# A third two-bank PSUM tile shared by scores and feed-forward units in a block-sparse attention and squared-ReLU kernel

## The chip, the cores and the metric

The kernel runs on one core of a Trainium2 chip. Its time is device microseconds of one execution. The core has a matrix engine (PE), which writes its results to PSUM; a vector engine (DVE) and a scalar engine (ACT), which read PSUM and write SBUF; a general engine (POOL), which works on SBUF; and a sequencer (SP), which issues transfers here. All run in parallel, each takes its own instructions in order, and semaphores order them among each other. PSUM has eight banks of 512 fp32 values per partition.

## The reference

```python
B, H, S, D = q.shape                       # 4, 8, 768, 64; blocks of 32, 24 of them
scores = scale * np.matmul(q, k.transpose(0, 1, 3, 2))
mask = np.abs(blk_i - blk_j) <= 1
mask = mask | (blk_i == 0) | (blk_j == 0) | (blk_i == n_blocks - 1) | (blk_j == n_blocks - 1)
for qb in range(n_blocks):
    for kb in sampled_blocks[qb]:
        mask[qb * block:(qb + 1) * block, kb * block:(kb + 1) * block] = True
scores = np.where(mask, scores, -1000000000.0)
...
x = softmax(scores) @ v                    # softmax written out in the reference
x = x.transpose(0, 2, 1, 3).reshape(B * S, H * D)     # 3072 x 512
h = x @ w_in                               # 512 x 2048
r = np.maximum(h, 0.0)
out = (r * r) @ w_out                      # 2048 x 512, result 3072 x 512
```

## The kernel before

**Attention.** Heads are taken in pairs, so there are 16 units `u` (4 batches of 4 pairs), and keys lie on the partitions. The work is cut into *slots*: a unit, a query tile and a group of key chunks of 128. In batch 0 the first 256 queries are two tiles of 128 with three key chunks per slot (16 slots in all); everywhere else a tile has 256 queries and a slot two key chunks. There are 148 slots. `scores` (L391) fills a slot's two-bank PSUM tile, one bank per head; its matmuls have only 64 rows, one half of the array for each head. In the narrow slots `scores` also adds the mask with a second matmul (L395). `exps` on ACT (L402) takes the tile to SBUF as `pT`; `masks` on DVE (L409) multiplies the 0/1 mask `MK` in; `values` (L431) accumulates `po`, whose 65th column is the softmax's sum; `normalize` (L439, L441) divides; a transpose, on PE in batch 0 and by DMA later, gives `xT`. Queries and keys are cast on DVE, POOL or ACT (L198 to L200) and transposed, on PE for batch 0 (`pt`, L343) and by DMA on SP's queue later (L350). The mask tiles `MK` are made on PE (`pk`, L313) and evacuated by DVE or ACT.

**Feed-forward.** Token tiles of 128, 128, 256 and 256 (batch 0) and of 384 (later) go through `hidden` (L485: `w_in` columns against `xT`, into `ph`), `relu` on ACT or DVE (L492, L494: PSUM to fp32 in SBUF), `square` on POOL or ACT (L503, L501: to bf16) and `output` (L526: into `py`), which ACT or DVE copies out and SP's queue stores. A *unit* of `hidden`, `relu` and `square` is one block of 128 hidden features, or two for the tiles of 128 tokens, so 256 or 384 wide.

**PSUM.** `ps_s` holds two tiles of two banks for scores, `ps_h` two single banks for `ph`, `pk`, `pt` and one in two of the last tile's outputs, `ps_o` one bank for `po`, `ps_y` one for `py`.

**Order.** Nothing runs in the order in which the code states it. Every piece of work is a task (`T_`) with durations per engine, a key, things it waits for, buffers that it takes (`get`) and gives back (`put`). `run_schedule` (L119) plays them on a clock of its own and always issues the task that can start first by that clock, ties by key; keys carry a small pseudo-random part (`TIES`, `SEEDS`). So each engine's order is fixed when the kernel is built, and at run time an engine that waits holds everything behind it. A *visit* is an uninterrupted stretch of score matmuls on PE. `attend` puts two slots in one visit, and in batch 0's narrow tiles one. From batch 1 on a visit isn't planned before a pace (`PACE0`, `PACE`). The weights come in eight pieces over POOL's queue (L365, L368), and two pieces of `w_out` gate batch 1's first loads (`GATES`, L375).

Of the kernel before, what the change touches and what calls it, by code (L numbers as in the profile page):

```python
# [25 lines left out]
def kernel(  # L26
# [27 lines left out]
    TWM = 384  # L54
# [5 lines left out]
    PT_BUFS, R_BUFS, G_BUFS, XT_BUFS = 6, 4, 2 * NF + 2, 3  # L60
# [3 lines left out]
    ps_s = ctx.enter_context(tc.psum_pool(name="ps_s", bufs=2))  # L64
    ps_o = ctx.enter_context(tc.psum_pool(name="ps_o", bufs=1))
    ps_h = ctx.enter_context(tc.psum_pool(name="ps_h", bufs=2))
# [9 lines left out]
    CB, GATES = 0.4, (6, 7)  # L76
    QT0, ADDED, ALONE = [(0, 128), (128, 128), (256, 256), (512, 256)], (0, 128), (0, 128)
# [5 lines left out]
    AHEAD = {"PE": 0.021, "DVE": 0.089, "ACT": 0.144, "POOL": 0.0, "SP": 0.0}  # L83
    LEAD = 9.733
    PACE0, PACE, SINGLE, MASK_AT = 43.352, 1.684, 1, 17.0

    class Buf:
        def __init__(self, pool):
            self.pool, self.holds, self.free = pool, 0, 0.0
# [4 lines left out]
    TIES = 2.757, 2.707  # L94
    SEEDS = (
            997007, 734824, 532673, 925841, 745989, 714641, 109461, 798098, 925326,
            634149, 527289, 224329, 653624, 743444, 608088, 229557, 928387, 381331,
            84432, 104783, 194889, 255966, 621276, 580226, 46894, 921115)
# [6 lines left out]
    class Task:  # L105
        def __init__(self, engs, key, fn, deps=(), get=(), put=(), after=0.0, mode=None, dma=0.0, late=None, bias={}, port=False):
            self.engs = engs if isinstance(engs, dict) else dict([engs])
            self.key, self.fn = key, fn
            self.deps, self.get, self.put = list(deps), list(get), list(put)
            self.after, self.mode, self.dma, self.late, self.bias = after, mode, dma, late, bias  # L110
            self.port = port
            self.end = self.eng = None
            self.order = len(tasks)
            self.key += TIES[0 if key < 300 else 1] * tie(self.order)
            for b in self.put:
                b.holds += 1
            tasks.append(self)

    def run_schedule(free, bufs, dma_free, mode=128):  # L119
        taken = {name: [] for name in bufs}  # L120
        port = {"DVE": (0.0, 0.0), "POOL": (0.0, 0.0)}
# [7 lines left out]

        while waiting or ready:  # L130
            now = [t for t in waiting if all(d.end is not None for d in t.deps)]
# [4 lines left out]
            found, urgent = [], {}  # L136
            for t in ready:
                r0 = t.after
                ok = True
                cnt = {}  # L140
                for b in t.get:
                    held = taken[b.pool]
# [10 lines left out]
                for e, us in t.engs.items():  # L153
                    r = max([r0, free[e]] + [seen(d, e) for d in t.deps])
# [6 lines left out]
                found.append((round(opt[1], 4), t.key, t.order, t, opt))  # L161
                if t.key < 100:
# [3 lines left out]
                       key=lambda c: c[:3], default=None)  # L166
            assert best is not None, "no task can start"
# [19 lines left out]
            for b in t.get:  # L187
                taken[b.pool].append(b)
# [65 lines left out]
    junk = ps_h.tile([P, 512], F32, name="junk", tag="h")  # L254
    for _ in range(N_WARM):
        nc.tensor.matmul(junk[:, 0:256], warm[:, 0:P], warm, start=True, stop=True)
# [45 lines left out]
    def mask_rows(c0, c1, e):  # L302
        mtile["R"] = ps_s.tile([P, 1024], F32, name="pb", tag="ps")[:, 0:c1 - c0]
# [7 lines left out]
    def mask_tile(n, c0, c1, e):  # L311
        pk = ps_h.tile([P, 512], F32, name="pk", tag="h")[:, 0:c1 - c0]
# [26 lines left out]
    def transp(u, w, ns, e):  # L339
        src = cast.pop((u, w, ns.start))  # L340
        pt = ps_h.tile([P, NCH, P], BF, name="pt", tag="h")
# [39 lines left out]
    def scores(slots, add, e):  # L381
        for a in slots:
            u, q0, w, cs = a
            i = u % NPB
            ps = ps_s.tile([P, 2, 512], F32, name="ps", tag="ps")
# [88 lines left out]

    def per_unit(T):
        return 2 if T[2] == P else 1

    def hidden(T, f, half, e):
        b, c0, w = T
        n = per_unit(T)  # L480
        if half == 0:
            htile[T, f] = ps_h.tile([P, TWM], F32, name="ph", tag="h")[:, 0:w * n]
        work_ = [(f + i, i, kc) for i in range(n) for kc in range(KM)]
        for f_, i, kc in work_[half * len(work_) // 2:(half + 1) * len(work_) // 2]:
            nc.tensor.matmul(htile[T, f][:, i * w:(i + 1) * w], w_in_sb[:, kc, f_ * P:(f_ + 1) * P], xT[b][:, kc, c0:c0 + w],  # L485
                             start=(kc == 0), stop=(kc == KM - 1))

    def relu(T, f, e):
        r = work.tile([P, TWM], F32, name="r", tag="r", bufs=R_BUFS)[:, 0:T[2] * per_unit(T)]
        src = htile.pop((T, f))  # L490
        if e == "ACT":
            A.activation(out=r, in_=src, func=AF.Relu)  # L492
        else:
            V.tensor_scalar(out=r, in0=src, scalar1=0.0, scalar2=None, op0=AOP.max)  # L494
        rltile[T, f] = r

    def square(T, f, e):
        g = work.tile([P, TWM], BF, name="g", tag="g", bufs=G_BUFS)[:, 0:T[2] * per_unit(T)]
        r = rltile.pop((T, f))
# [4 lines left out]
        for i in range(per_unit(T)):  # L504
            gtile[T, f + i] = g[:, i * T[2]:(i + 1) * T[2]]
# [12 lines left out]
    def y_pool(T, i):  # L518
        return "h" if T == TILES[-1] and i % 2 else "y"

    def output(T, i, ts, cs, part, e):
        if part == 0:
            pool, tag = (ps_h, "h") if y_pool(T, i) == "h" else (ps_y, "y")
            ytile[T, i] = pool.tile([P, d_model], F32, name="py", tag=tag)[:, 0:cs[1] - cs[0]]
# [14 lines left out]
    def T_(engs, key, f, *args, **kw):  # L539
# [5 lines left out]
              (3, 0, 0): 9.8, (3, 1, 0): 10.9, (1, 2, 0): 11.9, (2, 2, 0): 13.0, (3, 2, 0): 14.0}  # L545
    arrive.update({(u, 0, 2): (15.1, 15.8, 16.4, 17.1)[u] for u in range(HP)})
# [13 lines left out]
    def prepare(u):  # L560
# [17 lines left out]
        else:  # L578
            at = dict(after=arrive[u, 2, 0])
            late_q = first_of_tile[u, 2 * P]  # L580
            for w, ns in [(1, ns) for ns in (KEYS if u == 0 else (ALL,))] + [(0, ns) for ns in QRS]:
# [4 lines left out]
                qc, hb = Buf("qc"), Buf("h")  # L586
# [6 lines left out]
                t = T_(("PE", 0.06 * n), key + 1, transp, u, w, ns, deps=[c], get=[hb], put=[qc], mode=128)  # L593
# [12 lines left out]
    def attend(group, add):  # L606
        s = min(order.index(a) for a in group)
        bufs = {a: Buf("ps") for a in group}
# [3 lines left out]
        sc = T_(("PE", (0.44 if add else 0.22) * area), s, scores, group, add,  # L612
                deps=deps + (mr[:1 + (group[-1][1] + group[-1][2] > QW)] if add else []) + sc_all[-1:], get=[bufs[a] for a in group], mode=64,
                after=PACE0 + PACE * (s - N0) * (1.06 - 0.0006 * (s - N0)) if s >= N0 else 0.0)
        sc_all.append(sc)
        for a in group:
# [5 lines left out]
            ex = T_(("ACT", 0.2 + 0.82 * part), s, exps, a, deps=[sc], get=[pt], put=[bufs[a]])  # L622
# [4 lines left out]
            va = T_(("PE", 0.245 * part), s + 3.009, values, a, deps=[ex] + cv[u] + va_all[-1:] + (kws if po_pool(u, q0) == "y" else []),  # L627
# [23 lines left out]
    for i, (c0, c1) in enumerate(((0, QW), (QW, S))):  # L651
        rb_ = Buf("ps")
        t = T_(("PE", 0.11 + 0.11 * i), 5.0 if i else -90.0, mask_rows, c0, c1, after=9.8 if i else 4.6, get=[rb_], put=[], mode=32)
# [6 lines left out]
    for us in [range(b * HP, (b + 1) * HP) for b in range(B)]:  # L660
# [3 lines left out]
        if us[0] < HP:  # L664
            for c0, c1, at in MASKED:
                for n in range(NCH):
                    mb, w = Buf("h"), (c1 - c0) / 512
                    t = T_(("PE", 0.216 * w), (2 * n + 30 if c0 == 0 else 2 * n + 2), mask_tile, n, c0, c1, get=[mb], mode=128, after=at, deps=mr)
# [3 lines left out]
            while mine:  # L672
                q0 = mine[0][1]
                n = 1 if q0 in ALONE or len(mine) == 1 else 2
                attend(mine[:n], q0 in ADDED)
                mine = mine[n:]
        else:
            for i in range(0, len(mine) - 1, 2):
# [82 lines left out]
```

## Time and profile before

| what | value |
|---|---|
| median of 13 runs (lowest, highest) | 274.0 us (273.22, 276.55) |
| the profiled execution: its own time | 274.45 us |
| its span, first to last instruction | 272.7 us |
| busy: PE, ACT, DVE, POOL | 97%, 76%, 69%, 40% of the span |
| granted PE clock | 1.000 |
| scores to `pT` on ACT (L402), 128x1024 | 132 of 1022 ns |
| mask on DVE (L409) | 132 of 788 ns |
| relu of 384: on ACT (L492), on DVE (L494) | 46 of 497 ns, 50 of 556 ns |
| relu of 256: on ACT, on DVE | 35 of 404 ns, 13 of 420 ns |
| square of 384: on POOL (L503), on ACT (L501) | 62 of 963 ns, 34 of 525 ns |
| square of 256: on POOL, on ACT | 33 of 848 ns, 15 of 430 ns |
| output copy of 512 (L198, L200): on ACT, on DVE | 21 of 589 ns, 2 of 680 ns |

A mean is the length of one instruction from start to reported end. Neighbours on one engine overlap somewhat, so how many fit in a stretch is read from the distance of their starts. The end of a matmul is modelled, so a PE that is busy 97% of the time may still be held up; distances between starts show it.

### The profile page before, as it was taken

What the parts mean: (1) busy time and instruction counts of PE and PEld (TensorE: products, weight loads), DVE (VectorE), ACT (ScalarE), POOL (GpSimd) and SP (SyncE); (2) the same over time, 40 slices, a digit from 0 to 9 for tenths busy, and PEclk for the clock granted to TensorE, in tenths of its full rate; (3) what the DMA queues carried; (4) which work ended last, traced back from release to release, by engine and by line L of the source; (5) the groups of instructions that cost most, each with busy time, mean ns of one, the idle gap of its engine ahead of it and who ended that gap; (6) DMA issues with size and microseconds to landing.
All of it is one profiled execution on the core that took longest, in us unless ns stands there. A gap on an engine that the chain in (4) does not pass through costs nothing.

```text
span 272.7 us, 7435 instructions
## 1 busy us (share of the span) xinstructions
PE 263.6 (97%) x2994; PEld 164.1 (60%) x3032; DVE 189.5 (69%) x380; ACT 207.5 (76%) x321; POOL 110.2 (40%) x138
## 2 busy tenths in 40 slices
PE   8999999999999999999999999999999999999995
PEld 5778766667676555665556555556555555555544
DVE  6698879988786768889667877776666875434400
ACT  3798999999999879999998799889999881010111
POOL 3293453357446126444420270431411414666410
PEclk9999999999999999999999999999999999999999
DMA  6999998999991285399721133255210111111112
GB/s 193 372 225 201 206 279 267 293 295 335 200 231 22 94 140 165 74 258 249 209 58 51 53 76 71 58 108 60 67 52 19 51 20 51 38 40 41 38 71 83
DMA packets 51882, 36.92 MB, mean 135 GB/s; under 512 B 30984, under 2 KB 48904, under 8 KB 51848
## 3 DMA queue, kind: packets, MB, share of 16 engines
q1 hardware_dynamic: 47080, 31.86, 45.2%
q0 software_dynamic: 4224, 4.19, 9.7%
q8 instruction: 23, 0.38, 0.6%
q10 hardware_dynamic: 544, 0.39, 0.5%
q14 instruction: 11, 0.09, 0.1%
HBM read 27.26 MB, written 6.29 MB: 123 GB/s over the span
## 4 chain that ended last, share of the span: by engine, by line
PE 82%; DMA 11%; POOL 2%; ACT 2%; issue 1%; DVE 0%; SPq 0%; ACTq 0%
PE py L526 29%; PE ph L485 29%; PE po L431 12%; PE ps L391 12%; DMA w_out_sb<-in_moe_w_out_dram 6%; DMA vs<-in_v_dram 3%; DMA qs<-in_q_dram 2%; ACT pT L402 1%; POOL w_in_sb L365 1%; POOL w_out_sb L368 1%; ACT ys L198 0%; POOL VT L200 0%; PE pk L313 0%; ACT xT L198 0%; DVE pT L409 0%
## 5 line engine op out<-in xcount | busy, mean ns | idle before, releaser
L402 ACT ACTIVATE pT<-ps 128x1024 bf16<-128x1024 f32 (+1 forms) x148 | 140.2, 1000 | 11.8 <-PE ps L391 7.7
L503 POOL TENSOR_TENSOR g<-r 128x384 bf16<-128x384 f32 (+1 forms) x95 | 87.0, 923 | 121.1 <-DVE r L494 64.3
L409 DVE TENSOR_TENSOR pT<-pT,MK 128x1024 bf16<-128x1024 bf16 x132 | 102.2, 788 | 16.4 <-ACT pT L402 15.9
L485 PE MATMUL ph<-xT,w_in_sb 128*128 128x384 bf16 (+2 forms) x640 | 106.4, 294 | 0.1
L526 PE MATMUL py<-w_out_sb,g 128*128 128x512 bf16 (+1 forms) x362 | 94.2, 370 | 2.6 <-issue 0.5
L485 PEld LDWEIGHTS <-w_in_sb 128*128 128x128 bf16 x640 | 52.0, 97 | 28.7 <-issue 5.0
L431 PEld LDWEIGHTS <-pT 128*128 128x128 bf16 x1152 | 47.3, 98 | 17.3 <-issue 4.1
L494 DVE TENSOR_SCALAR r<-ph 128x384 f32<-128x384 f32 (+1 forms) x63 | 33.1, 528 | 31.4 <-PE ph L485 28.8
L431 PE MATMUL po<-VT,pT 128*128 128x65 bf16 x1152 | 53.7, 193 | 0.5 <-DVE pT L409 0.3
L526 PEld LDWEIGHTS <-g 128*128 128x128 bf16 x400 | 36.2, 98 | 28.6 <-issue 3.1
L391 PE MATMUL ps<-QK 64*128 64x256 bf16 (+1 forms) x624 | 47.6, 265 | 0.6 <-ACT pT L402 0.5
L198 ACT COPY ys<-py 128x512 f32<-128x512 f32 (+1 forms) x23 | 13.1, 570 | 38.0 <-PE py L526 37.8
L391 PEld LDWEIGHTS <-QK 64*128 64x128 bf16 x624 | 25.1, 95 | 23.0 <-issue 19.6
L492 ACT ACTIVATE r<-ph 128x384 f32<-128x384 f32 (+1 forms) x81 | 34.3, 457 | 3.0 <-PE ph L485 2.8
L501 ACT ACTIVATE g<-r 128x384 bf16<-128x384 f32 (+1 forms) x49 | 24.1, 496 | 6.0 <-DVE r L494 4.8
L200 POOL CAST VT<-vs 128x768 bf16<-128x768 f32 x15 | 13.9, 925 | 24.6 <-PE po L431 14.5
L441 DVE TENSOR_TENSOR xq<-po,rs 128x256 bf16<-128x256 f32 (+1 forms) x52 | 21.0, 404 | 1.8
L439 DVE RECIPROCAL rs<-po 128x4 f32<-128x4 f32 (+1 forms) x52 | 9.1, 176 | 13.6 <-PE po L431 13.2
L200 DVE CAST qc<-qs 128x768 bf16<-128x768 f32 (+2 forms) x18 | 11.7, 652 | 0.3 <-DMA qs<-in_q_dram 0.3
L200 DVE CAST qc<-ks 128x768 bf16<-128x768 f32 (+1 forms) x15 | 9.0, 603 | 2.3 <-DMA ks<-in_k_dram 2.2
L395 PE MATMUL ps<-R,oh 64*128 64x128 bf16 x96 | 7.1, 223 | 0.0
L343 PE MATMUL pt<-identb,qc 128*128 128x128 bf16 x48 | 5.3, 234 | 0.7 <-DVE QK L200 0.6
(51 smaller groups left out, 64.0 us busy)
## 6 DMA issues: line engine op xcount, KB each, us to landing
vs<-in_v_dram SPq DMA_DIRECT2D x16, 384.0 KB, 6.7
out_dram<-ys SPq DMA_DIRECT2D x23, 256.0 KB, 2.1
ks<-in_k_dram SPq DMA_DIRECT2D x15, 384.0 KB, 5.1
qs<-in_q_dram SPq DMA_DIRECT2D x12, 384.0 KB, 4.4
w_in_sb<-in_moe_w_in_dram POOLq DMA_DIRECT2D x4, 512.0 KB, 8.8
w_out_sb<-in_moe_w_out_dram POOLq DMA_DIRECT2D x4, 512.0 KB, 16.5
qs<-in_q_dram SPq DMA_DIRECT2D x4, 256.0 KB, 7.3
xT<-xq SPq DMA_TRANSPOSE x36, 2.3
```

What stands on the lines that cost most here:

```text
L200: (V if e == "DVE" else G).tensor_copy(out=out, in_=in_)
L391: nc.tensor.matmul(ps[:, h, j * w:(j + 1) * w], QK[i][hs, 1, ksl], QK[i][hs, 0, qsl], start=j == 0, stop=not add, skip_group_check=True)
L402: A.activation(out=pT[:, :, 0:n], in_=stile.pop(a)[:, :, 0:n], func=AF.Exp, scale=scale)
L409: V.tensor_tensor(out=pT, in0=pT, in1=m[:, None].broadcast_to([P, 2, len(cs), w]), op=AOP.mult)
L431: nc.tensor.matmul(po[:, qc, h, :], pT[:, h, j * w + qc * P:j * w + (qc + 1) * P], VT[i][:, h, n, 0:VW], start=(n == 0 and qc == 0 and h = ...
L441: V.tensor_tensor(out=xq, in0=po[:, :, :, 0:D], in1=rs.broadcast_to([P, n, 2, D]), op=AOP.mult)
L485: nc.tensor.matmul(htile[T, f][:, i * w:(i + 1) * w], w_in_sb[:, kc, f_ * P:(f_ + 1) * P], xT[b][:, kc, c0:c0 + w], start=(kc == 0), stop= ...
L492: A.activation(out=r, in_=src, func=AF.Relu)
L494: V.tensor_scalar(out=r, in0=src, scalar1=0.0, scalar2=None, op0=AOP.max)
L501: A.activation(out=g, in_=r, func=AF.Square)
L503: (G if e == "POOL" else V).tensor_mul(out=g, in0=r, in1=r)
L526: nc.tensor.matmul(ytile[T, i], gtile[T, f][:, ts * P:(ts + 1) * P], w_out_sb[:, f, cs[0]:cs[1]], start=(f == 0), stop=(f == NF - 1))
```

## The change

*PSUM.* `ps_s` and `ps_h` go. There are two tiles X0 and X1 of two banks from the start, and two single banks F0 and F1, which hold the transposes, mask tiles, mask rows and the first two tiles' hidden units in the opening. When no task is left that needs a single bank, F0 and F1 are given up and become a third two-bank tile X2. Scores' slots, hidden units of the other token tiles and every second output of the last tile take any free X tile.

*Units.* A unit is 512 wide in batch 0 (four feature blocks of 128 tokens or two of 256) and 768 later (two of 384), and `relu` takes it in one instruction across two banks. Squares are 512 or, two to a unit, 384 wide. The buffers for squares are still 34, now up to 512 wide instead of 384; the four relu buffers are 768 wide.

*Visits.* `GROUPS` says how many slots a visit has, by batch and query third: (1, 2, 2), (2, 2, 2), (2, 2, 3), (3, 3, 3). An exp may be planned before the whole visit's scores are done (`lead`).

*Planner.* It places X tiles (`bank`), holds hidden units back where a visit is due and tiles are short (`yields`, `paced`), and has other constants and seeds: `PACE0` 40.119 instead of 43.352, values' key s + 1.282 instead of s + 3.009, other arrival times. So every engine's order changes. The computation doesn't.

```diff
-    TWM = 384
+    TWM = 768
-    PT_BUFS, R_BUFS, G_BUFS, XT_BUFS = 6, 4, 2 * NF + 2, 3
+    PT_BUFS, R_BUFS, G_BUFS, XT_BUFS = 6, 4, 34, 3
-    ps_s = ctx.enter_context(tc.psum_pool(name="ps_s", bufs=2))
+    ps_x = ctx.enter_context(tc.psum_pool(name="ps_x", bufs=1))
-    ps_h = ctx.enter_context(tc.psum_pool(name="ps_h", bufs=2))
+    GROUPS = (1, 2, 2), (2, 2, 2), (2, 2, 3), (3, 3, 3)
-    PACE0, PACE, SINGLE, MASK_AT = 43.352, 1.684, 1, 17.0
+    PACE0, PACE, SINGLE, MASK_AT = 40.119, 1.714, 1, 17.0
...
+        def bank(pool, now):
+            n, best = (1, None) if pool == "X1" else (2, None)
+            for c in (4, 5) if pool == "X1" else (0, 2) if singles else (0, 2, 4):
+                mine = [cells[i] for i in range(c, c + n)]
+                if c in gone or any(b and b.holds for b in mine):
+                    continue
+                r = max([now] + [b.free for b in mine if b])
+                k_ = (round(max([now] + [b.free + 0.8 for b in mine if b]), 4), c)
+                if best is None or k_ < best[0]:
+                    best = (k_, c, r)
+            return best
...
+                if t.yields and not relaxed and due - HOLD < opt[1] and spare <= len(paced[0].get):
+                    continue
...
+    X = [ps_x.tile([P, 1024], F32, name=f"X{i}") for i in range(2)]
+    FB = [ps_f.tile([P, 512], F32, name=f"F{i}") for i in range(2)]
+    def pair_of(b):
+        if b.at == 4 and len(X) == 2:
+            first_pool.__exit__(None, None, None)
+            X.append(ctx.enter_context(tc.psum_pool(name="ps_z", bufs=1)).tile([P, 1024], F32, name="X2"))
+        return X[b.at // 2]
...
     def per_unit(T):
-        return 2 if T[2] == P else 1
+        return {P: 4, QW: 2, S // 2: 2}[T[2]]
...
-            A.activation(out=r, in_=src, func=AF.Relu)
+            A.activation(out=to, in_=src, func=AF.Relu)
...
-        bufs = {a: Buf("ps") for a in group}
+        bufs = {a: Buf("X2") for a in group}
...
-            ex = T_(("ACT", 0.2 + 0.82 * part), s, exps, a, deps=[sc], get=[pt], put=[bufs[a]])
+            ex = T_(("ACT", 0.2 + 0.82 * part), s, exps, a, deps=[sc], lead=sc.engs["PE"] * (len(group) - 1 - i) / len(group), get=[pt], put=[bufs[a]])
...
-            va = T_(("PE", 0.245 * part), s + 3.009, values, a, ...
+            va = T_(("PE", 0.245 * part), s + 1.282, values, a, ...
...
+        while mine:
+            n = min(len(mine), GROUPS[us[0] // HP][mine[0][1] // QW])
+            if n == 3:
+                n = sum(a[:2] == mine[0][:2] for a in mine)
+            attend(mine[:n], us[0] < HP and mine[0][1] in ADDED)
+            mine = mine[n:]
```

## The prediction

> **What bounds the kernel now.** I read the page first, then the busy time by stretches, the waits, and the timeline of single engines.
>
> ```profile
> span 272.7 us, 7435 instructions
> PE 263.6 (97%) x2994; PEld 164.1 (60%) x3032; DVE 189.5 (69%) x380; ACT 207.5 (76%) x321; POOL 110.2 (40%) x138
> ...
> ACT  3798999999999879999998799889999881010111
> ```
>
> PE looks full all the way, but a busy PE need not be a PE at its peak, so I ask which engines are full in which stretch: the opening up to the first 256-wide scores, the rest of batch 0, batches 1 to 3 while scores run, and what follows the last scores. Columns are stretch and length, then busy us (count) of PE, PEld, DVE, ACT, POOL, then granted clock, DMA share, GB/s.
>
> ```profile
> 6.30:23.50 17.20, 16.28 (x347) 12.95 (x348) 13.69 (x44) 14.30 (x24) 9.26 (x13) 1.00 1.11 281
> 23.50:58.50 35.00, 33.31 (x495) 24.25 (x502) 29.32 (x60) 33.63 (x60) 15.63 (x18) 1.00 1.12 267
> 58.50:222.00 163.50, 161.76 (x1850) 97.48 (x1878) 123.67 (x227) 149.00 (x222) 61.89 (x64) 1.00 0.51 116
> 222.00:272.70 50.70, 47.14 (x285) 25.98 (x288) 18.26 (x35) 8.41 (x15) 21.26 (x26) 1.00 0.14 50
> ```
>
> From 23.5 to 58.5 ACT is busy 96%, as full as PE; later it is at 91%, and PE alone is full. The waits say the same: evacuating engines wait for PE, PE hardly for them (total us, times, longest).
>
> ```profile
> DVE r L494 <- PE ph L485: 28.8, 35, 2.6
> ...
> DVE pT L409 <- ACT pT L402: 15.9, 23, 1.3
> ...
> PE ps L391 <- ACT pT L402: 0.5, 2, 0.3
> ```
>
> The price of each kind of PE work is read from where the next group starts (start, length, x count).
>
> ```profile
> 90.19 0.61 PE L391 MATMUL ps<-QK 64*128 64x256 bf16 x8
> 90.73 0.42 PE L431 MATMUL po<-VT,pT 128*128 128x65 bf16 x8
> 90.99 1.46 PE L526 MATMUL py<-w_out_sb,g 128*128 128x512 bf16 x6
> 92.28 0.41 PE L431 MATMUL po<-VT,pT 128*128 128x65 bf16 x8
> 92.52 0.59 PE L526 MATMUL py<-w_out_sb,g 128*128 128x512 bf16 x2
> 93.05 0.61 PE L391 MATMUL ps<-QK 64*128 64x256 bf16 x8
> ```
>
> Six 512-wide matmuls take 1.29 us (0.216 each), eight 65-wide 0.24-0.26 (0.030 each). Two 512-wide ahead of scores take 0.53: 0.43 plus 0.10. Eight score matmuls take 0.54; they run in pairs, one per head, so four times 0.109, plus 0.10 again. So each entry to the 64-row scores and each exit costs 0.096 us: **0.19 us per visit**. By widths, 128 columns cost 0.056, 256 0.109, 384 0.162.
>
> With these prices I add up all 3,032 matmuls in program order: hidden 83.2 us (384 of 384, 128 of 256, 128 of 128 columns), output 83.0, values 34.9, scores 34.0, visits 78 x 0.192 = 15.0, transposes, mask tiles and warm-up 8.6, together 258.7 us of pure PE work before. The last matmul ends at 269.4, so 10.7 us are lost. Setting each visit's start against its running sum tells where: 3.9 us ahead of the first scores (6.3), 2.5 up to 23.5, 2.7 up to 58.5, and 1.5 spread evenly over the 53 visits after that, 0.03 each, which is rounding of my prices and no wait. From 58.5 us on **PE doesn't wait at all**; nothing that only shortens other engines can gain there. After the last matmul come 3.3 us of copy and store.
>
> **The change, part by part.**
>
> *Fewer visits.* In program order scores are visited 78 times before and 72 times after: 12 becomes 14 in the opening (its slots are single more often), and 66 visits of two slots become 42 of two and 16 of three. Six fewer at 0.19 is **-1.15 us**; the same sum over the changed order is 257.5 us. Matmuls are the same in number and shape, so PE gains nothing else.
>
> *Batch 0's second half (the 2.7 us).* In these 12 visits ACT carries 32.3 us of work before, and PE 32.3: 24 exps at 0.90 from start to start (two take 1.93 in the timeline, one 1.02), 20 relus of 256 at 0.26, 10 squares at 0.32, four mask tiles at 0.28, output copies. Equal loads on in-order engines that feed each other leave waits. After, the first 11 visits carry 24.7 us of ACT against 27.2 of PE: five relus and two squares of 512 at 0.48 and 0.53 in place of most of the narrow ones, and less feed-forward work there. A stretch of 10.2 us of PE work without a new visit follows (ACT 7.9). One other stop here is the output projection at L526 that stands until 37.1 us for the third w_out piece to land; in the changed order the pieces go out 0, 1, 2, 3 instead of 0, 2, 1, 3, so f 4 to 7 arrive one piece sooner. The gate for batch 1's first loads now waits for the third-landing piece, 2.5 us later, which the 10.2 us cover: batch 1's first visit is due at about 62 us, not 58.5. If that cover fails, all visits of batch 1 shift. I take half of the 2.7 back: **-1.3 us**, bounds 0 and -2.7.
>
> *Opening.* Same input loads; DVE gets four mask tiles (0.34 each) and a 512 copy from ACT, ACT loses them. DVE has 13.7 of 17.2 us busy, so I take 0, bounds -0.5 and +1.
>
> *Wider relus and squares.* 144 relus (96 of 384, 48 of 256) become 72 (48 of 768, 24 of 512). The widths 512 and 768 aren't in the trace as relus. On ACT the rows of 256 and 384 go 0.264 and 0.370 from start to start, 0.106 per 128, so 0.48 and 0.69; with nothing saved they would be two narrow ones, 0.53 and 0.74. On DVE 0.34 and 0.475 give 0.61 and 0.88 (at most 0.68 and 0.95). I take the lower ends, whose slope the rows show; 48 times 0.05 is 2.4 us of ACT that PE covers either way. They lie beside PE work. They free their banks later, though. The Trainium skill speaks against this: its page "Perfetto Trace Analysis", section "Optimizing Scalar/DVE Operations", says that where ACT and DVE aren't saturated but cause bubbles elsewhere, instructions should be broken up so that work completes sooner. A 768 relu holds its tile 0.3 us longer than a 384 one (0.80 against 0.50 to its end); were each of the 48 exposed, that is +14 us. The row decides otherwise as long as PE has other work: evacuation waited 28.8 us for PE, PE 0.5 for evacuation. I take 0 and check it on a cycle.
>
> *A three-slot cycle by hand* (batch 3, order: 12 scores, 4 output, 6 hidden, 8 values, 2 hidden, 2 output, 8 values, 2 output; PE 4.35 us). Time 0 is the first score matmul. An idle exp starts 0.43 after it, so exps end at 1.45, 2.36, 3.26; masks 0.03 later plus 0.69: 2.17, 3.08, 3.98. PE leaves scores at 0.75, outputs until 1.61: the first tile is free (1.45). Hidden to 2.58, values of slot one (2.17, slack 0.4), hidden to 3.15. Its relu starts 3.42, when ACT is free (3.14), ends 4.22. Values of slot two at 3.58 (3.08, slack 0.5). The next scores start 4.35 and write the relu's tile last, at 4.79: slack 0.5. The DVE also has an output copy (0.68) in some cycles, behind the first mask: mask two then ends at 3.4, slack 0.2. Two-unit cycles are 5.89 us on PE against ACT 5.4 at most. For the stages: batch 1's visits need ACT 32.9 and DVE 29.6 in 36.3 us of PE, batch 2's 38.7 and 30.8 in 48.3, batch 3's 62.8 and 44.2 in 75.6; the worst run of visits where an engine exceeds PE is 0.3 us (ACT) and 0.8 (DVE). So new waits: **+0.5**, bounds 0 and +4.
>
> *Tail.* Same last 512- and 256-wide outputs; ACT takes 12 wide relus (19 us of its work in 43). 0.
>
> Sum: 272.7 - 1.15 - 1.3 + 0.5 = 270.7 for the span. The profiled execution took 274.45 with 272.7 of span, and the median of the 13 runs is 274.0; I take the change of -2.0 to the median: **272.0 us**.
>
> **Rivals.**
>
> *Nothing but the visits, and new waits eat them.* The opening's 2.7 us come from data arriving, not from ACT; for it speaks that 2.5 us more were lost before 23.5 with ACT at only 83%. Then -1.15 + 0.5 to +1.2 gives 273.4, range 272.9 to 274.6.
>
> *Slower: masks late in three-slot cycles.* DVE and POOL slow each other: the mask takes 0.69 at the median but up to 1.33, and two together 1.92 where squares run on POOL (100.97 us). A mask late by 0.64 exceeds the 0.2 to 0.5 slack; PE then stands at the values (L431), and with it everything, as values now follow scores sooner (key s + 1.3, not s + 3.0). At 0.3 per visit in the 15 three-slot cycles that is +4.5, with only the visits gained: 274.0 - 1.15 + 4.5 = 277.4; at half of that 275.1. It decides above 0.16 us per visit, where it eats the 2.45 gained. Against it: POOL has fewer squares (62 of 384 and 33 of 256 become 49 and 13 of 512).
>
> *The whole opening gain, no new wait:* 274.0 - 1.15 - 2.7 = 270.2.
>
> **How the numbers follow.** My sum 50% (own range 270.9 to 272.9); nothing but the visits 22%; slower by late masks 18%; whole gain 10%. About 0.3% (0.8 us: 273.2 and 274.8) is what a measurement tells from no change. Faster: 50 + 10 + 3 of the second; slower: 17 of the third and 2 of the second; same: the rest. Range: 270.3 leaves about 8% below, 275.4 about 12% above.
>
> **What would show it.** Right: PE's waits for ACT and DVE stay below 1 us past 60; the first-to-last distance of batch 3's visits is that of its PE work; the stretch before 60 us shows ACT less full; wide relus near 0.80 and 0.97. Wrong: PE rows for values that wait for the mask (L474 after) by some us, gaps ahead of scores that wait for a relu, or batch 1's first scores waiting for a transposed load around 60 us.

## The result and the profile after

The changed kernel takes 271.75 us in the median of 11 runs (271.07 to 273.2), the kernel before 274.02 us in 48 runs; the ratio is 0.9918, with a 95% interval from 0.9898 to 0.9938. That is 2.2 us less (1.7 to 2.8), where 2.0 less was forecast. A twelfth execution, at 274.53 us with a mean granted clock of 0.993, is not in this median; with it the median is 271.9 us. The profiled execution of the changed kernel is its fastest, 271.07 us with a span of 269.3, so the two spans (272.7 and 269.3) differ by more than the medians do: the profiled execution of before lies 0.4 us above its median, that of after 0.7 below.

The page of the changed kernel, its busy time and the tenths of ACT over the span:

```profile
span 269.3 us, 7318 instructions
...
PE 260.8 (97%) x2993; PEld 165.1 (61%) x3032; DVE 177.1 (66%) x349; ACT 216.8 (81%) x285; POOL 86.5 (32%) x109
...
ACT  3788999978998998998786798999988978645511
```

PE is as full as before. ACT has 36 instructions less and yet 9 us more of work, because more of the relus and squares go to it; DVE and POOL have 12 and 24 us less. The last fifth of ACT's row now holds the wide relus of the tail, as the prediction said.

The same stretches as before (stretch and length, then busy us and count of PE, PEld, DVE, ACT, POOL, then granted clock, DMA share, GB/s):

```profile
6.30:23.50 17.20, 16.59 (x340) 12.17 (x338) 14.67 (x46) 13.86 (x22) 8.97 (x12) 1.00 1.13 290
23.50:58.50 35.00, 34.54 (x531) 26.26 (x535) 30.65 (x62) 32.13 (x45) 16.56 (x14) 1.00 1.09 262
58.50:219.00 160.50, 157.91 (x1792) 96.80 (x1821) 119.76 (x213) 142.04 (x177) 46.93 (x51) 1.00 0.49 120
219.00:269.30 50.30, 46.60 (x306) 26.20 (x310) 7.52 (x13) 26.62 (x40) 11.56 (x14) 1.00 0.14 46
```

From 23.5 to 58.5 us ACT falls from 96% to 92% and PE rises from 95% to 99%. The waits (total us, times, longest) have the same shape as before, with evacuating engines waiting for PE and hardly the reverse:

```profile
DVE pT L474 <- ACT pT L467: 24.6, 46, 2.0
...
ACT r L563 <- PE X L554: 14.1, 22, 1.7
...
PEld L496 <- DVE pT L474: 3.2, 14, 0.5
...
PE X L456 <- ACT pT L467: 0.2, 1, 0.2
```

The third line is the one that grew: weight loads of the values wait for masks 3.2 us in 14 places. In the kernel before it was:

```profile
PEld L431 <- DVE pT L409: 2.1, 9, 0.4
```

A three-slot cycle of batch 3, as it ran (start, length, instructions of a group):

```profile
167.59 0.83 PE L456 MATMUL X<-QK 64*128 64x256 bf16 x12
168.58 0.81 PE L598 MATMUL py<-w_out_sb,g 128*128 128x512 bf16 x3 [0.16 <-issue]
169.23 1.14 PE L554 MATMUL X<-xT,w_in_sb 128*128 128x384 bf16 x6
170.21 0.41 PE L496 MATMUL po<-VT,pT 128*128 128x65 bf16 x8
170.45 1.79 PE L554 MATMUL X<-xT,w_in_sb 128*128 128x384 bf16 x10
172.07 0.65 PE L496 MATMUL po<-VT,pT 128*128 128x65 bf16 x16
172.56 1.02 PE L598 MATMUL py<-w_out_sb,g 128*128 128x512 bf16 x4
173.52 0.39 PE L456 MATMUL X<-QK 64*128 64x256 bf16 x4
```

5.93 us from scores to scores, against 5.89 of priced work, and no engine in brackets: PE stops nowhere in it. (One matmul of 512 columns ahead of 168.58 has no record; its time stands there as idle.) The next cycle has the order that the prediction laid by hand; it takes 4.38 us (173.52 to 177.90), where 4.35 was forecast.

To place the change I use the prediction's measure again: the start of each visit less the running sum of the priced matmuls in program order, which is the time lost up to there. Each program has its own sum (258.7 us before, 257.5 after); the rows are those of single executions, the kernels of later sections among them, where their program is the same up to the column's end.

| us lost | to the first 256-wide scores | from there to batch 1's first scores | from there to the last scores |
|---|---|---|---|
| before | 6.4 | 2.70 | 1.52 |
| after | 5.6 | 1.01 | 1.76 |
| before, w_out pieces in the other order | 5.6 | 2.08 | 1.51 |
| before, batch 0's squares on POOL | 6.3 | 3.36 | 1.52 |
| after, visits broken | 6.5 | 1.28 | - |
| after, masks of batch 3 twice | 5.9 | 1.22 | - |
| after, batch 2's squares on POOL | 7.8 | 1.14 | 1.98 |
| after, narrow relus | 5.9 | 1.03 | 2.48 |
| after, ACT loaded in batch 0 | 6.2 | 2.44 | 1.76 |

The first column scatters from execution to execution in both programs (5.6 to 6.4, and 5.6 to 6.5 with one at 7.8), so the 0.7 us between the two profiles there can't be put down to the change. The last repeats best: it is 1.51 to 1.52 in all three programs of before and 1.76 in two of after; the middle one is 1.01 to 1.28 in the four rows of the changed kernel whose program is the same there. So the gain lies in the visits (1.15 us less work) and in batch 0's second half (1.5 us, from 2.70 to 1.16 as the mean of those four rows); 0.24 us is given back later.

### The profile page after: what moved, and what is told of

It is laid out like the page before. It is cut to its first block, busy times and chain, and to the rows that moved or that the text cites. A ratio compares the mean times of both kernels' runs of the same rounds, so it can differ in the third digit from the quotient of the medians.

```text
span 269.3 us, 7318 instructions
## 1 busy us (share of the span) xinstructions
PE 260.8 (97%) x2993; PEld 165.1 (61%) x3032; DVE 177.1 (66%) x349; ACT 216.8 (81%) x285; POOL 86.5 (32%) x109
## 4 chain that ended last, share of the span: by engine, by line
PE 88%; DVE 3%; DMA 3%; SPq 2%; issue 2%; ACT 1%; POOL 1%; ACTq 0%
PE X L554 28%; PE py L598 27%; PE po L496 14%; PE X L456 13%; PE F L554 3%; DMA vs<-in_v_dram 3%; DVE pT L474 2%; PE X L598 2%; SPq L278 2%; ACT pT L467 1%; PE F L378 1%; PE po L513 1%; DVE xq L506 0%; PE X L460 0%; POOL w_in_sb L430 0%
## 5 line engine op out<-in xcount | busy, mean ns | idle before, releaser
L467 ACT ACTIVATE pT<-X 128x1024 bf16<-128x1024 f32 (+1 forms) x148 | 138.7, 1004 | 13.3 <-PE X L456 8.3
L575 POOL TENSOR_TENSOR g<-r 128x384 bf16<-128x384 f32 (+1 forms) x62 | 57.2, 927 | 143.0 <-ACT r L563 102.5
L554 PE MATMUL X<-xT,w_in_sb 128*128 128x384 bf16 (+1 forms) x512 | 90.1, 313 | 0.0
L563 ACT ACTIVATE r<-X 128x768 f32<-128x768 f32 (+1 forms) x48 | 37.0, 773 | 15.4 <-PE X L554 14.1
L456 PE MATMUL X<-QK 64*128 64x256 bf16 (+1 forms) x624 | 46.1, 263 | 0.3 <-ACT pT L467 0.2
L573 ACT ACTIVATE g<-r 128x384 bf16<-128x384 f32 (+1 forms) x58 | 31.2, 544 | 7.0 <-DVE r L565 5.7
L565 DVE TENSOR_SCALAR r<-X 128x768 f32<-128x768 f32 (+1 forms) x16 | 13.4, 838 | 11.5 <-POOL g L575 7.9
L252 DVE COPY ys<-py 128x512 f32<-128x512 f32 x12 | 8.2, 684 | 17.8 <-PE py L598 11.0
L250 ACT COPY ys<-py 128x512 f32<-128x512 f32 (+1 forms) x11 | 6.3, 572 | 6.3 <-PE py L598 6.3
L554 PE MATMUL F<-xT,w_in_sb 128*128 128x128 bf16 x128 | 8.7, 219 | 0.1
```

The costliest lines, as they stand in the source:

```text
L252: (V if e == "DVE" else G).tensor_copy(out=out, in_=in_)
L456: nc.tensor.matmul(ps[:, h, j * w:(j + 1) * w], QK[i][hs, 1, ksl], QK[i][hs, 0, qsl], start=j == 0, stop=not add, skip_group_check=True)
L467: A.activation(out=pT[:, :, 0:n], in_=stile.pop(a)[:, :, 0:n], func=AF.Exp, scale=scale)
L554: nc.tensor.matmul(htile[T, f][:, i], w_in_sb[:, kc, (f + i) * P:(f + i + 1) * P], xT[b][:, kc, c0:c0 + w], start=(kc == 0), stop=(kc == K ...
L563: A.activation(out=to, in_=src, func=AF.Relu)
L565: V.tensor_scalar(out=to, in0=src, scalar1=0.0, scalar2=None, op0=AOP.max)
```

## The experiments

Every ratio below is to the kernel before, run beside the experiment; as us it is taken of 274.3, and set against the changed kernel's -2.2. In edited kernels the line numbers are higher by one to three.

**What a visit costs.** In each three-slot visit a one-column matmul of 128 rows is put between the slots.

```diff
             ps = pair_of(bufs[a]).rearrange("p (h c) -> p h c", h=2)
+            if len(slots) == 3 and a != slots[0]:
+                nc.tensor.matmul(ps[:, 0, 0:1], warm[:, 0:P], warm[:, 0:1], start=True, stop=True)
```

> The changed kernel, with one matmul of 128 rows and one column put between the slots of each three-slot visit, so that 32 more visits are made and nothing else is different. If a visit costs 0.19 us on a PE that never waits, as the working has it: 32 x (0.192 + 0.03 to 0.06 for the extra matmul and its weights) = +7.1 to +8.1 us, so about 279 to 280 us. If the price of a visit is partly a wait for something else that the regrouping did not take away, or if PE has slack in these cycles: under +4 us, so under 276 us.

Measured: 279.07 us, ratio 1.0193 (1.0155 to 1.0231), so 7.5 us above the changed kernel. PE's timeline of one visit:

```profile
152.64 0.39 PE L458 MATMUL X<-QK 64*128 64x256 bf16 x4
152.96 0.18 PE L452 MATMUL X<-warm 128*128 128x1 bf16 x1
153.07 0.39 PE L458 MATMUL X<-QK 64*128 64x256 bf16 x4
153.40 0.18 PE L452 MATMUL X<-warm 128*128 128x1 bf16 x1
153.50 0.39 PE L458 MATMUL X<-QK 64*128 64x256 bf16 x4
```

Slots start 0.43 us apart, where two matmul pairs take 0.217: the exit and entry cost 0.21 with the small matmul in them. The first three-slot visit starts at 147.78 us and the last matmul ends at 274.00; in the changed kernel it is 146.64 and 266.02. So from there to the end this run takes 6.8 us more, for 32 added visits, 0.21 each. The price of a visit is paid in full, and the six visits saved are worth 6 x 0.19.

**Narrow relus on the same tiles.**

```diff
-        if e == "ACT":
-            A.activation(out=to, in_=src, func=AF.Relu)
-        else:
-            V.tensor_scalar(out=to, in0=src, scalar1=0.0, scalar2=None, op0=AOP.max)
+        for i in (slice(0, n // 2), slice(n // 2, n)):
+            if e == "ACT":
+                A.activation(out=to[:, i], in_=src[:, i], func=AF.Relu)
+            else:
+                V.tensor_scalar(out=to[:, i], in0=src[:, i], scalar1=0.0, scalar2=None, op0=AOP.max)
```

> The changed kernel, with each relu made as two instructions of half its width on the same tile (2 x 384 for 768, 2 x 256 for 512); order, tiles and visits stay. If PE covers ACT and DVE, as the working has it: 72 more fixed costs of about 0.05 us on ACT and 0.07 on DVE stay hidden, 0 to +0.5 us, so 271.8 to 272.3 us. If the wide relus hold PE up, as the rule on breaking up long instructions would have it, halves of the same tile do not free it sooner either, so this run can only show what width itself costs; if ACT is at its limit in the three-slot cycles: +1.5 us or more, so over 273.2 us.

Measured: 272.94 us, ratio 0.9956 (0.9938 to 0.9974), 1.0 us above the changed kernel, twice the upper end of what I expected. The table has 0.72 of it past batch 1's first scores. The groups of the changed kernel (count, then busy us and mean ns of one, then idle time and what ended most of it):

```profile
L563 ACT ACTIVATE r<-X 128x768 f32<-128x768 f32 x39 | 31.6, 813 | 14.1 <-PE X L554 13.0
...
L565 DVE TENSOR_SCALAR r<-X 128x768 f32<-128x768 f32 x9 | 8.6, 954 | 10.3 <-POOL g L575 7.9 <-PE X L554 2.4
```

and of this run:

```profile
L564 ACT ACTIVATE r<-X 128x384 f32<-128x384 f32 x78 | 34.0, 492 | 13.5 <-PE X L554 12.3
```

A pair of 384 ends some 0.05 us later than one of 768 (0.37 and 0.69 from start to start). ACT is not full, but the small delays reach PE; at which of the 72 places was not looked up. The order was planned for wide relus, so this is what halving them costs here, not what narrow tiles cost in a plan of their own.

**Is ACT's room what gained in batch 0?** First, the changed kernel with ACT filled up again.

```diff
+        if a[0] < HP and a[1] >= QW and a[3][0] % 4 == 0:
+            A.activation(out=load_to, in_=place[:, 0:256], func=AF.Square)
         A.activation(out=pT[:, :, 0:n], in_=stile.pop(a)[:, :, 0:n], func=AF.Exp, scale=scale)
```

> The changed kernel, with one extra ACT square of 256 columns on scratch ahead of every other exp of batch 0's slots from column 256 on: 12 x 0.32 = 3.8 us of ACT put back, so that ACT's and PE's loads are as equal there as before the change (about 28 us each over the first 11 visits). If equal loads were what lost the 2.7 us before: 1.3 to 2.7 us come back, so 273 to 274.5 us, lost between 23 and 61 us. If data arrival or the order of the weight pieces was the cause: under +0.6 us, so under 272.4 us.

Measured: 273.29 us, ratio 0.9964 (0.9941 to 0.9988), 1.3 us above the changed kernel. The condition takes two of three key pairs, so it added 16 squares, not 12, each 0.52 us long. The stretch of batch 0's second half, within half a microsecond, in this run, and in the changed kernel:

```profile
22.60:62.60 40.00, 39.43 (x577) 29.22 (x574) 32.81 (x70) 38.88 (x66) 16.86 (x15) 1.00 1.10 258
```

```profile
22.60:61.01 38.41, 37.88 (x564) 28.68 (x567) 33.38 (x69) 34.66 (x50) 17.46 (x15) 1.00 1.12 264
```

ACT is busy 97% instead of 90%, and 1.3 us are lost (2.44 against 1.16 in the table). So the changed kernel does need ACT's room, at least ahead of exps, where the added squares stand. Does its lack explain the kernel before? There the same relief was tried: the 15 squares of batch 0 that ran on ACT go to POOL at their places.

```diff
-        if e == "ACT":
+        if e == "ACT" and T[0]:
             A.activation(out=g, in_=r, func=AF.Square)
         else:
-            (G if e == "POOL" else V).tensor_mul(out=g, in0=r, in1=r)
+            (G if e in ("ACT", "POOL") else V).tensor_mul(out=g, in0=r, in1=r)
```

> The kernel before, with the 15 squares of batch 0 that ran on ACT put on POOL at their places; order of all else stays. ACT gets 15 x 0.32 = 4.8 us less between 25 and 75 us, most of it before 58 us. If equal loads of ACT and PE lose the 2.7 us: 0.7 to 1.5 us come back, 272.5 to 273.3 us. If it is data arrival or the order of the pieces: within 0.3 us of before. POOL's squares may slow masks on DVE, which would take some of the gain back.

Measured: 275.18 us, ratio 1.003 (1.0012 to 1.0048): slower by 0.8 us. The stretch in this run:

```profile
23.50:58.50 35.00, 33.29 (x484) 23.85 (x489) 30.75 (x60) 30.61 (x50) 21.74 (x26) 1.00 1.12 272
```

ACT falls from 33.63 to 30.61 us, lower than in the changed kernel, and PE gains nothing. But the run is not a clean test, as one place shows. In the kernel before, scores wait there for an exp:

```profile
30.74 0.39 PE L391 MATMUL ps<-QK 64*128 64x256 bf16 x4
31.44 0.39 PE L391 MATMUL ps<-QK 64*128 64x256 bf16 x4 [0.30 <-ACT pT L402]
```

From start to start that stop is 0.5 us. With the squares on POOL 0.1 of it is left, so ACT's relief did work:

```profile
30.68 0.69 PE L391 MATMUL ps<-QK 64*128 64x256 bf16 x8
31.55 0.65 PE L431 MATMUL po<-VT,pT 128*128 128x65 bf16 x16 [0.18 <-DVE xT L200]
```

Right behind it, though, values lose 0.54 us at two places (31.55 and 32.50), where DVE is late: the two masks there take 0.97 and 1.02 us beside the moved squares, where each took 0.69 before, and the copy of `xT` between them comes later as well. All in all the visits stand within 0.2 us of where they stood up to 52 us, and then 0.8 us are lost in one of them, where values wait for an evacuation on DVE. The masks from 23 to 62 us take 0.89 us on average, against 0.83. So moving squares to POOL doesn't help, because DVE pays for it; what relief of ACT alone is worth in the kernel before is not shown, beyond the 0.4 us of this one stop.

**The order of the weight pieces.** In the kernel before, the second and third piece of w_out change places, gates with them.

```diff
     def w_load(i, e):
+        i = {5: 6, 6: 5}.get(i, i)
...
     def loads_gate(i, e):
+        i = {5: 6, 6: 5}.get(i, i)
```

> The kernel before, with the second and third piece of w_out loaded in the other order (0, 1, 2, 3, as in the changed kernel), and nothing else changed. If the order of the pieces is a part of the 1.3 us won in batch 0's second half: the stop of the output projection until 37.1 us goes and 0.5 to 1.0 us come back, 273.0 to 273.5 us where the kernel before takes 274.0, with the distance of the visits at 34.3 and 37.6 us shortened. If ACT's load alone lost the 2.7 us: PE waits for ACT at once where it waited for the piece, under 0.3 us.

Measured: 273.76 us, ratio 0.9975 (0.9956 to 0.9994), 0.7 us faster. The place where the kernel before stood until 37.1 us, there and here:

```profile
37.08 0.38 PE L526 MATMUL py<-w_out_sb,g 128*128 128x512 bf16 x1 [0.46 <-DMA w_out_sb<-in_moe_w_out_dram]
```

```profile
34.97 0.89 PE L487 MATMUL ph<-xT,w_in_sb 128*128 128x128 bf16 x12
35.69 0.38 PE L528 MATMUL py<-w_out_sb,g 128*128 128x512 bf16 x1
36.22 0.39 PE L393 MATMUL ps<-QK 64*128 64x256 bf16 x4
```

The output projection starts without a wait, and the stretch loses 2.08 us instead of 2.70; the 0.62 are kept to the end (1.51 after it as before). This is the largest single piece of the gain in batch 0. What else was lost there before were single stops, from start to start: 0.5 us at the scores that wait for an exp (31.4 us), 0.42 and 0.26 at values behind late masks (44.8 and 58.1), 0.2 each at two transposes and an output. The new order has two of 0.26 and 0.34 us in their place. Which of its parts (tiles, widths, keys) removes which stop was not told apart.

**Late masks, by their own time.** Each mask of batch 3 is multiplied in twice.

```diff
-        V.tensor_tensor(out=pT, in0=pT, in1=m[:, None].broadcast_to([P, 2, len(cs), w]), op=AOP.mult)
+        for _ in range(2 if u >= 3 * HP else 1):
+            V.tensor_tensor(out=pT, in0=pT, in1=m[:, None].broadcast_to([P, 2, len(cs), w]), op=AOP.mult)
```

> The changed kernel, with each of the 36 masks of batch 3 multiplied in twice (the mask is zeros and ones, so the values stay): +0.6 us of DVE per slot, +1.8 per three-slot cycle. If the cycle laid by hand is right, slot one's mask comes 0.2 us and slot two's 0.4 us after its values are due, so the 12 three-slot cycles of batch 3 lose about 0.4 us each: +4.8 us, so about 276.5 us (range 275 to 278). If there is more slack in the program's own order than in the cycle laid by hand: under +1.5 us, so under 273.3 us. If the masks were already at the edge, as the rival of late masks has it: over +7 us, so over 279 us.

Measured: 293.72 us, ratio 1.0714 (1.0686 to 1.0742), 21.8 us above the changed kernel. Of 36 x 0.6 = 21.6 us of added DVE time about 20 reach the end (a fall of the clock, told at the end, adds 1.7 in the profiled execution), though DVE is busy only 77% from 147 to 225 us of that run. One cycle:

```profile
181.44 0.83 PE L456 MATMUL X<-QK 64*128 64x256 bf16 x12
182.55 0.42 PE L497 MATMUL po<-VT,pT 128*128 128x65 bf16 x8 [0.28 <-DVE pT L475]
182.80 1.03 PE L599 MATMUL py<-w_out_sb,g 128*128 128x512 bf16 x4
183.66 1.14 PE L555 MATMUL X<-xT,w_in_sb 128*128 128x384 bf16 x6
185.36 0.42 PE L497 MATMUL po<-VT,pT 128*128 128x65 bf16 x8 [0.56 <-DVE pT L475]
...
188.61 0.65 PE L497 MATMUL po<-VT,pT 128*128 128x65 bf16 x16 [1.65 <-DVE pT L475]
189.19 0.50 PE L456 MATMUL X<-QK 64*128 64x256 bf16 x6
```

The values of slots two and three (188.61) stand ahead of the next scores in PE's queue. So scores, exps, three masks in series and values form a loop, and what a mask is late is late for the next scores as well. In the changed kernel I set each mask's end against the start of its values: the shortest distance is 0.06 us, which is the latency where PE waits, and the middle one 0.43; slot one has 0.29 to 0.43 in all 16 visits. The slack laid by hand (0.2 to 0.5) is about right. What I had wrong is what happens beyond it: I let each cycle lose 0.4, and it lost 1.8, 1.6 without the fall of the clock.

**Late masks, by POOL.** The rival's own mechanism: the 18 squares of batch 2 that ran on ACT are put on POOL, by the same edit as above with T[0] != 2 in place of T[0].

> The changed kernel, with the 18 squares of batch 2's feed-forward tiles that ran on ACT put on POOL at their places, so that POOL works beside the masks of the three-slot cycles (in the changed kernel the masks there take 0.688 us on average and 0.69 at most; in the kernel before, with more squares on POOL, 0.79 and 1.33). Masks reach PE with only about 0.06 us of latency and 0.2 to 0.4 us of slack before their values are due. If a mask late by up to 0.64 us stops PE, as the rival of late masks has it: 18 squares at 0.1 to 0.4 us lost each, +2 to +6 us, 273.5 to 277.5 us. If the cycles absorb it, or the masks are not slowed: under +0.8 us, under 272.5 us.

Measured: 272.54 us, ratio 0.9928 (0.9903 to 0.9953), 0.3 us above the changed kernel and within the intervals. The masks of the stretch from 145 to 222 us, before and after:

```profile
L409 DVE TENSOR_TENSOR pT<-pT,MK 128x1024 bf16<-128x1024 bf16 x49 | 37.8, 785 | 7.7 <-ACT pT L402 7.7
```

```profile
L474 DVE TENSOR_TENSOR pT<-pT,MK 128x1024 bf16<-128x1024 bf16 x47 | 31.8, 688 | 12.9 <-ACT pT L467 12.9
```

Before, 27 of 49 masks ran beside a POOL instruction and 14 were slowed, by 5.2 us together. After, one of 47 ran beside one, and none was slowed. With 18 squares more on POOL 9 of 47 meet one and 3 are slowed (0.97 to 1.31 us). Those three began while a square had 0.4 to 0.8 us to go; of the others four began in a square's last 0.2 us and two ahead of it. Of the three, the two in the visit at 159.4 us hold PE up, by 0.2 us. So the rival's price per late mask was not too high, but masks and squares rarely meet in this order.

**Two-slot visits in the changed kernel.**

```diff
-    GROUPS = (1, 2, 2), (2, 2, 2), (2, 2, 3), (3, 3, 3)
+    GROUPS = (1, 2, 2), (2, 2, 2), (2, 2, 2), (2, 2, 2)
```

> The changed kernel with two-slot visits throughout batches 1 to 3, scheduled anew: the third two-bank tile and the wide relus stay, the three-slot visits go. 80 visits instead of 72; its matmuls in program order sum to 259.0 us of PE work against 257.5. If fewer visits are a gain by themselves: +1.5 us, about 273.3 us (up to 274.3 with stops of the new order). If the three-slot visits bring waits that eat their gain, so that the change lives from the wide tiles: within 0.5 us, 271.3 to 272.3 us.

Measured: 277.85 us, ratio 1.0108 (1.0072 to 1.0144), 5.2 us above the changed kernel. Only 1.5 of it are visits. The order that comes out puts two visits in a row (145 and 147 us) beside almost no feed-forward work: 4.04 us of PE against 4.5 of ACT, with a wide relu on DVE ahead of the masks. 1.9 us are lost there, and then the clock falls. Windows of this run:

```profile
147.97:151.38 3.41, 1.89 (x34) 1.28 (x32) 2.87 (x5) 2.40 (x4) 0.60 (x1) 1.00 0.04 13
151.38:154.79 3.41, 3.19 (x21) 1.51 (x19) 1.39 (x2) 1.94 (x2) 0.00 (x0) 0.50 0.27 83
```

After 3.4 us in which PE was busy 1.9, the granted clock is halved for 3.41 us, which costs another 1.6. The three executions of eight with a mean clock of 0.999 or 1.0 took 275.4 to 275.9 us, the five with 0.992 to 0.994 277.4 to 278.8. As a test of the visits alone the run is inconclusive: what it shows is what one badly filled pair of visits costs.

**More three-slot visits.** First in batches 1 and 2 as well.

```diff
-    GROUPS = (1, 2, 2), (2, 2, 2), (2, 2, 3), (3, 3, 3)
+    GROUPS = (1, 2, 2), (3, 3, 3), (3, 3, 3), (3, 3, 3)
```

> The changed kernel, with three-slot visits in batches 1 and 2 too (all thirds), scheduled anew: 62 visits instead of 72. If PE has nothing to wait for from 60 us on and a visit costs 0.19 us: 10 x 0.192 = -1.9 us, about 269.8 us. If the waits of three-slot cycles (masks with 0.2 to 0.4 us of slack) bite where batch 1's cycles hold less feed-forward work: no gain or slower, 271.5 to 275 us.

Measured: 288.98 us, ratio 1.0517 (1.0481 to 1.0553), 16 us above the changed kernel. PE's timeline in batch 1, and ACT's exps of the same cycle:

```profile
79.87 0.83 PE L456 MATMUL X<-QK 64*128 64x256 bf16 x12
80.63 0.66 PE L496 MATMUL po<-VT,pT 128*128 128x65 bf16 x16
82.66 0.42 PE L496 MATMUL po<-VT,pT 128*128 128x65 bf16 x8 [1.37 <-DVE xq L506]
83.01 0.83 PE L456 MATMUL X<-QK 64*128 64x256 bf16 x12
...
80.31 2.85 ACT L467 ACTIVATE pT<-X 128x1024 bf16<-128x1024 f32 x3 [0.34 <-PE X L456]
```

These cycles hold scores and values alone, 1.6 us of PE, and last 3.1, because three exps take 2.8 on ACT. From 73 to 98 us eight cycles lose 11.7 us. Then batch 2 alone, with the scores due later and wider apart, so that each cycle had its share of feed-forward work:

```diff
-    GROUPS = (1, 2, 2), (2, 2, 2), (2, 2, 3), (3, 3, 3)
+    GROUPS = (1, 2, 2), (2, 2, 2), (3, 3, 3), (3, 3, 3)
...
-    PACE0, PACE, SINGLE, MASK_AT = 40.119, 1.714, 1, 17.0
+    PACE0, PACE, SINGLE, MASK_AT = 41.5, 1.8, 1, 17.0
```

> The changed kernel with three-slot visits in all of batch 2 too, and the scores' due times set 1.4 us later and 5% wider apart, so that no cycle is scheduled with less feed-forward work than its exps last: the largest run of cycles in which ACT's work exceeds PE's is 0.8 us, against 0.3 in the changed kernel and 20 us or so in the run with three-slot visits in batch 1 too, whose cycles of three slots with values alone stood 3.1 us each for 3 exps of 0.9. 68 visits, 256.7 us of PE work. If feed-forward work beside the exps is what a three-slot visit needs: -0.8 us and up to +0.8 of new stops, 271.0 to 271.8 us. If three-slot visits are bad in themselves where batch 1 and 2 meet: over 273 us.

(The expectation's "20 us or so" for the run before it is wrong: the largest excess of ACT's work over PE's there, added up as for the others, is 10.3 us.) Measured: 277.19 us, ratio 1.0121 (1.0081 to 1.0161), 5.6 us above the changed kernel. From batch 1's first scores to the last it loses 7.6 us instead of 1.76, in a dozen stops of 0.1 to 1.0 us at values and outputs. So enough work in each cycle is not sufficient, and my explanation of the run before is incomplete; what makes one order of three-slot cycles tight and another loose stays open. Neither version beats the changed kernel.

**The order without its noise.** Both kernels add a fixed noise to the planner's keys. Setting it to zero leaves the order to the keys (first edit in the kernel before, second in the changed one).

```diff
-    TIES = 2.757, 2.707
+    TIES = 0.0, 0.0
...
-    TIES = 3.944, 4.402
+    TIES = 0.0, 0.0
```

> The kernel before with the scheduler's tie noise set to zero, so that the order is that of the keys alone: 81 visits, 259.2 us of PE work (258.7 with the noise), ACT never more than 0.8 us ahead of PE's work. If its order with the noise was much better than chance: 275.5 to 278 us. If the noise is worth little: 274 to 275 us.

> The changed kernel with the scheduler's tie noise set to zero: 73 visits, 257.7 us of PE work, and one run of cycles in batch 1 in which ACT's work exceeds PE's by 1.7 us. If the change's gain lies in its structure (fewer visits, wide tiles): 1.5 us or more below the run of the kernel before without noise, about 272.5 to 274 us. If it lies in the order that the noise happened to give: no faster than the kernel before without noise.

Measured: 277.28 us (1.011, 1.0082 to 1.0138) for the kernel before and 274.81 us (1.0018, 0.9999 to 1.0037) for the changed one. The noise of each kernel is worth about 3 us to it, more than the change is. Without it the change gains 2.5 us (0.9%), with it 2.2 (0.8%), so the total does not hang on one order. Its parts do. PE's sums without noise, 259.2 and 257.7 us, give 1.5 of the 2.5: fewer visits pay in both pairs of orders. Batch 0's second half gives only 0.25 there (1.68 and 1.43 us lost, by the table's measure), and from batch 1's first scores on 0.4 is given back (4.22 and 4.63). The rest stands ahead of the first 256-wide scores, 1.4 us in the two profiles; as single executions of one program scatter by 0.8 us and more there, how much of it is the change's is not known. So what is shown to come from the structure is the visits' gain; the 1.5 us of batch 0 belong to the two orders with noise. PE does not stop for a w_out piece in the kernel before without noise.

## Why the prediction was right, point by point

- *Fewer visits, -1.15 us*: right. The count of matmuls and visits is the program's own, and 0.21 us per added visit, paid in full, confirms the price.
- *Batch 0's second half, -1.3 us*: right in size (-1.5), partly wrong in cause, and in part luck. The figure was half of the 2.7 us by guess, and without the planner's noise the same step gives 0.25. The step put equal loads of ACT and PE first. Filling ACT again does cost the changed kernel 1.3 us, so the room is needed; but in the kernel before only one stop of 0.5 us waits for ACT. The order of the w_out pieces, which I named second, is worth 0.6 to 0.7 by itself, and masks slowed beside POOL another 0.7. The premise that failed is that equal loads as such lose the time: in the kernel before it was lost at places that can be listed, most of them not ACT's. What ACT's relief alone would give there stays open.
- *The 10.2 us without a new visit and batch 1's first scores at about 62 us*: they come at 60.9, and the later gate costs nothing that shows.
- *Opening 0*: right within its scatter. The 0.7 us that the two profiles differ by there is within the scatter of single executions.
- *Wider relus, 0*: too low. Their lengths were right (0.80 and 0.97 forecast, 0.81 and 0.95 measured), but halving them costs 1.0 us, so ACT's and DVE's time isn't free where PE is full. The advice of the Trainium skill that I weighed ("Perfetto Trace Analysis", section "Optimizing Scalar/DVE Operations": breaking up instructions may help where ACT and DVE, not saturated, cause bubbles elsewhere) was rightly set aside: PE waits 0.2 us for an exp in the whole span and for no relu, and the +14 us did not come. The run with halves does not test it, as both halves must end before the tile is free.
- *New waits, +0.5*: +0.24 measured, none of them in the three-slot cycles, which lose 0.03 us each.
- *Tail 0*: right. From the last scores to the last matmul both kernels lose 0.15 us over their priced work.
- *Rivals*: that only the visits count was wrong by the table's second column. Late masks in three-slot cycles were rightly feared (1.6 to 1.8 us per cycle when they take twice their time) and wrongly placed: where these cycles run one mask of 47 meets a POOL instruction and none is slowed. That I gave it 18% rested on mask lengths of the kernel before, and those belong to that kernel's order.

## What to carry to other kernels

Price what each kind of work costs on the full engine, add it up in program order, and set it against the trace's starts: the difference says where time is lost, and past batch 1's first scores it repeated to 0.01 us between executions here. Before blaming two equally full engines for a loss, list the stops; they may be a weight piece out of order or a late mask, and each can be tried alone. A group of dependent work between two instructions of the bounding engine's queue is a loop: within its slack a delay costs nothing, beyond it every cycle pays nearly all of it (20 of 21.6 us here). And when a planned order is compared with another, take the planner's noise out of both: a total may stay while its parts move.

## What the runs showed of the hardware

- The granted clock halved for 3.41 us in the midst of two profiled executions, each time after an equally long stretch with PE busy 1.89 us (two-slot visits, shown there) and 1.48 (masks twice, first windows below). The Trainium skill, "TensorE: Matmul & The Clock Gate", section "What's actually happening", gives the same window of 3.41 us and ties the fall to an idle window; here PE was far from idle in both. In the run with three-slot visits in batch 1 two windows on the clock's own grid (its records change at whole steps of 3.41 us) had PE busy 1.81 and 1.80 us, less than the 1.89, and the clock stayed at 1.00 (second windows). So the busy share read from the trace does not decide it alone.

```profile
193.94:197.35 3.41, 1.48 (x22) 0.81 (x20) 3.34 (x7) 2.11 (x4) 0.77 (x1) 1.00 0.12 40
197.35:200.77 3.42, 3.42 (x18) 1.31 (x17) 1.42 (x3) 2.39 (x3) 0.00 (x0) 0.50 0.84 77
```

```profile
90.55:93.96 3.41, 1.81 (x36) 1.34 (x36) 3.16 (x6) 3.16 (x4) 0.00 (x0) 1.00 0.12 24
93.96:97.37 3.41, 1.80 (x37) 1.34 (x36) 2.82 (x7) 3.12 (x4) 1.50 (x2) 1.00 0.78 144
```

- One such window takes 0.5 x 3.41 of some 270 us, 0.006, from the mean clock. By that estimate the execution of the changed kernel at 0.993 had one, and two of the six with three-slot visits in batch 1 (0.982) had three each; they have no trace.
- A mask of 1,024 elements per partition takes 0.68 to 0.69 us alone. In the kernel before, from 60 to 225 us, 24 masks began while a POOL square had at least 0.15 us to go; each ended 0.54 to 0.56 us after that square's end, and took 0.77 to 1.33 us. The 30 that began ahead of the POOL instruction beside them took 0.68 to 0.69. So it is the order of their starts that decides whether a mask is late.
